# A decoding pass that writes back in place, and a planner that counts a locked pass in full

## The chip, the cores and the metric

The kernel runs on one core of one Trainium2 chip. The metric is the device time of one execution in microseconds (us). Three executions of the kernel before took 615.13, 615.44 and 616.31 us; the median is 615.44.

## What is computed

The reference chains a chunked linear recurrence with decay (a state-space layer) and two dense feed-forward layers:

```python
for c in range(nc):                       # attention part, per batch and head
    cum = np.cumsum(la, axis=-1)
    M = np.einsum('bhin,bhjn->bhij', Cc, Bc) * np.exp(cum_i - cum_j) * causal
    y = np.einsum('bhij,bhjd->bhid', M, xc) + (Cc @ state) * np.exp(cum)
    state = decay_full * state + sum_j(Bc_j xc_j decay_from_j)
x = y as 3072 tokens x 256
h = x @ w_in;  x = (h * sigmoid(1.702 * h)) @ w_out       # first layer, 256 -> 2048 -> 256
h = x @ w_in2; x = (h * clip(h + 3, 0, 6) / 6) @ w_out2   # second layer
```

Everything is in float32.

## The kernel before

**Tiling.** The sequence is cut into 8 chunks of 96 steps. A chunk c has 4 pieces, one per batch, so there are 32 pieces q = 4c + b. A piece needs two decay scans on VectorE (`decay`, L387), eight small matmuls for the scores (`s_mm`, L458, named S below), two products scores times decay (`g_mul` on VectorE, L461, or `g_copy` on ScalarE and `g_pool` on GpSimd, L464 and L468), sixteen small matmuls (`y_mm`, L479, named Y), and then `y_out` on ScalarE (L487) and `y_lo` on VectorE (L492), which write the piece into a token block `xt`.

The two feed-forward layers go over seven token blocks of 384 or 480 columns (A is the first layer, B the second). The inner loop has 16 units m per block and layer; a unit is four plus two matmuls `l1` (L615) and six `l2` (L654). Every float32 operand is split into a rounded high part and the rest, so that three products are summed: `wh` and `wl` for a weight, `gh` and `gl` for an activation. The first twelve units are all of block 0; after them block 0 and block 1 alternate, so block 1 (pieces q4 to q7) must be there when unit 12 is under way.

**Weights.** There are 32 weight tiles p, one per unit and layer. They arrive as 64-bit words and are decoded on the chip in five steps:

- `w_load` (L295): a DMA of 512 KB into one of three buffers `raw`, as pairs of a low and a high 32-bit word.
- `w_scale` (L300, ScalarE): the high words, scaled, are written to one of two buffers `dec`.
- `w_low` (L305, VectorE): the low words are shifted, in place in `raw`.
- `w_join` (L309, VectorE): `dec` shifted and joined with the low words, in place in `dec`. It is the last reader of `raw`.
- `w_top` (L312, ScalarE) writes `wh` from `dec`; `w_bottom` (L318, GpSimd) writes `wl` from `dec` and `wh`. It is the last reader of `dec`.

**What sets the order.** The order of all instructions on the five engines comes out of the planner `Schedule`. Each operation is added with an engine, a planned duration, a due time (`key`), what it reads and writes (`r`, `w`) and which pool buffer it takes (`new`). `run` goes through planned time and takes on each engine the ready operation with the earliest due time. An operation that takes a buffer can't be planned before that buffer is free. An operation with `port=True` on VectorE, and each one on GpSimd, is lengthened in the plan if the other engine is in such an operation at that time. On the chip every engine and SyncE, which issues nearly all DMAs, go through their lists strictly in order, each instruction waiting for semaphores.

Of the kernel before, what the change touches and what calls it, by code (L numbers as in the profile page):

```python
# [8 lines left out]
F32 = mybir.dt.float32  # L9
# [5 lines left out]
AF = mybir.ActivationFunctionType  # L15
ALU = mybir.AluOpType
# [60 lines left out]
class Schedule:  # L77
# [12 lines left out]
    def add(self, eng, dur, key, fn, *args, r=(), w=(), new=(), kb=0, after=0.0, port=False):  # L90
        self.ops.append(dict(eng=eng, dur=dur, key=key, fn=fn, args=args, r=list(r), w=list(w) + list(new),
                             new=list(new), kb=kb, port=port or eng == "POOL", n=len(self.ops), ready=max(after, key - 8) if kb else after))
# [5 lines left out]
    def run(self):  # L98
# [39 lines left out]
        port = {"DVE": 0.0, "POOL": 0.0}  # L138
        pipe = 0.0
        order = []  # L140
        while any(cand.values()):
            best = None
            for e, cs in cand.items():
                run = []
                for o in cs:
                    t, need = max(at[e], o["ready"]), {}
                    for x in o["new"]:
                        p = x.split(":")[0]
                        need[p] = need.get(p, 0) + 1
                    for p, k in need.items():  # L150
                        f = sorted(free[p])
                        mine = set(turn[p][:k]) <= set(o["new"])
                        t = max(t, f[k - 1][0]) if mine and len(f) >= k else None
# [7 lines left out]
                t, k, n, o = min((x for x in run if x[0] <= t0 + 0.02), key=lambda x: x[1:3])  # L161
                for x in sorted(run, key=lambda x: x[1:3]):

                    if x[1] + 3 < k and x[0] <= t + min(0.4 * o["dur"], 0.5):
                        t, k, n, o = x
# [5 lines left out]
            t, n, o = best  # L171
            e = o["eng"]
            cand[e].remove(o)
            for x in o["new"]:
                f = free[x.split(":")[0]]
# [4 lines left out]
            if o["port"]:  # L180

                other = "DVE" if e == "POOL" else "POOL"
                o["dur"] += (0.45 if e == "POOL" else 0.6) * max(0.0, min(port[other] - t, o["dur"]))
                port[e] = t + o["dur"]
            at[e] = t + o["dur"]
            if o["kb"]:
# [25 lines left out]
def ssd_moe_kernel(ctx: ExitStack, tc: tile.TileContext, xs, aa, bc, bcz_d, bc0, wu, pat, idn, out):  # L212
    nc = tc.nc
# [3 lines left out]
    add = sch.add  # L217
# [39 lines left out]
    def B_(x):  # L257
        p = x.split(":")[0]
        return {"raw": raw_b, "dec": dec_b, "l": l_b, "gm": gm_b, "xs": xs_b, "st": st_b, "xt": xt_b, "gg": gg_b,
                "gh": gh_b, "gl": gl_b, "r16": r16_b, "lx": lx_b, "scr": scr_b, **banks}[p][sch.slot[x]]  # L260
# [19 lines left out]
    tu, t = [], START  # L280
# [8 lines left out]
    for q in range(NC * NB):  # L289
        k = max(i for i in range(NK) if LO[i] <= CH * q)  # L290
# [6 lines left out]
    def w_scale(p):  # L297


        nc.scalar.activation(B_(f"dec:{p}").bitcast(F32), B_(f"raw:{p}")[:, :, 1].bitcast(F32), AF.Prelu,  # L300
                             scale=2.0 ** 16, alpha=2.0 ** 32)

    def w_low(p):
        low = B_(f"raw:{p}")[:, :, 0]
        nc.vector.tensor_scalar(low, low, 29, None, ALU.logical_shift_right)  # L305

    def w_join(p):
        t = B_(f"dec:{p}")
        nc.vector.scalar_tensor_tensor(t, t, 3, B_(f"raw:{p}")[:, :, 0], ALU.logical_shift_left, ALU.bitwise_or)  # L309

    def w_top(p, e):
        (e.copy if e is nc.scalar else e.tensor_copy)(w_hi[p], B_(f"dec:{p}").bitcast(F32))  # L312
# [203 lines left out]
    for q in range(NC * NB):  # L516
        c, b = divmod(q, NB)
        t = kp[q]
        blk, f = block[q]
        if c in ROWS and b == 0:  # L520
            sch.take(rname(c), t - 5 if c else -75)
            rows[c] = []
            for i in range(4):
                for s in range(2) if c != 1 else (None,):
                    e = "SP" if c or s else "ACT"
                    n = f"r16.{c}.{i}.{s}"
                    add(e, 0.84 if c > 1 else 0.42, t - 4 if c else -70 + i, r16_load, {"SP": nc.sync, "ACT": nc.scalar}[e], c, i, s,
                        r=[rname(c)], w=[n], kb=115 if c == 1 else 57)
# [61 lines left out]
    for p in range(2 * NM):  # L590
        k = tu[first[p]] - 1.5
        R, Dn = f"raw:{p}", f"dec:{p}"
        n0 = 2 * NM - LATE
        add("SP", 0.4, k - 9, w_load, p, new=[R], kb=512, after=(2.9, 4.9, 6.9)[p] if p < 3 else 0.0)
        add("ACT", 0.72, k - 1.6, w_scale, p, r=[R], new=[Dn])
        add("DVE", 0.45, k - 1.9, w_low, p, w=[R], port=True)
        add("DVE", 0.70, k - 1.0, w_join, p, r=[R], w=[Dn], port=True)
        e = TOP(p)
        add(e, {"ACT": 0.64, "DVE": 0.43, "POOL": 1.0}[e], k - 0.5, w_top, p, ENG[e], r=[Dn], w=[f"wh{p}"])
        late_r, late_w = ["late"] * (p > n0), ["late"] * (p == n0)  # L600
        e = BOT(p)
        add(e, {"DVE": 0.78, "POOL": 1.3}[e], k, w_bottom, p, ENG[e], r=[Dn, f"wh{p}"] + late_r, w=[f"wl{p}"] + late_w, port=True)
# [174 lines left out]
```

## Time and profile before

| | |
|---|---|
| median of three executions | 615.44 us (615.13 to 616.31) |
| the profiled execution | 615.93 us, of which the span of the profile is 614.1 us |
| PE (TensorE matmul) busy | 601.0 us, 98% |
| VectorE (DVE) busy | 310.4 us, 51% |
| ScalarE (ACT) busy | 310.3 us, 51% |
| GpSimd (POOL) busy | 207.1 us, 34% |
| DMA | 53.69 MB, mean 87 GB/s |

TensorE is busy nearly all of the span, so time can be won or lost only where it stands still or runs at a lower granted clock. A stretch of the timeline shows for each instruction its start, its length and, in square brackets, how long its engine stood idle before it and what ended that wait. The lengths of VectorE and GpSimd include time in which the instruction was issued and not yet let through.

### The profile page before, as it was taken

To read this page: it belongs to the slowest core of one execution; us is meant where nothing else is said; L and a number is where in the kernel's file an instruction comes from. 1 tells how busy PE (TensorE), PEld (TensorE's weight loads), DVE (VectorE), ACT (ScalarE), POOL (GpSimd) and SP (SyncE) were. 2 spreads that over 40 slices of the span, in tenths; PEclk is the share of its full clock that TensorE was granted. 3 is DMA by queue.
4 is the path that set the end of the run, shared out by engine and by line. 5 is a ranking of instruction groups with operands and counts; after the bars stand their busy time and mean duration, and the time that the engine had idled before them with its cause. 6 is when DMAs were issued, how large, how long until landed. Compare 5 with 4: busy or idle time off the path is not lost.

```text
span 614.1 us, 9456 instructions
## 1 busy us (share of the span) xinstructions
PE 601.0 (98%) x3628; PEld 530.6 (86%) x3628; DVE 310.4 (51%) x466; ACT 310.3 (51%) x624; POOL 207.1 (34%) x176
## 2 busy tenths in 40 slices
PE   9787999999999999999999999999999999999997
PEld 7676998999998898788888888888888899988997
DVE  5979988654564777533545533644423222232222
ACT  3556666666555444444544446344445444444443
POOL 3646413264352551002750005550004430044453
PEclk9889899999999999999999999999999999999999
DMA  8676644434114492340425301903000010000000
GB/s 227 139 221 220 184 152 130 143 103 143 57 42 130 152 245 61 104 122 1 122 52 149 112 2 29 234 1 119 1 0 1 0 34 2 0 1 1 32 2 26
DMA packets 46781, 53.69 MB, mean 87 GB/s; under 512 B 27296, under 2 KB 38160, under 8 KB 46736
## 3 DMA queue, kind: packets, MB, share of 16 engines
q1 hardware_dynamic: 45888, 52.74, 30.0%
q10 hardware_dynamic: 848, 0.35, 0.3%
q8 instruction: 28, 0.46, 0.3%
q14 instruction: 17, 0.14, 0.1%
HBM read 42.01 MB, written 10.60 MB: 86 GB/s over the span
## 4 chain that ended last, share of the span: by engine, by line
PE 93%; DMA 2%; DVE 2%; ACT 1%; issue 1%; POOL 0%; SPq 0%; ACTq 0%; DVEq 0%; POOLq 0%
PE h L615 43%; PE acc L654 43%; PE s L458 2%; PE y L479 2%; PE acc L375 1%; DMA late<-in_bc 1%; PE s L479 1%; DMA raw<-in_wu 1%; DVE dec L309 1%; DVE l L387 1%; PE h L458 1%; PE acc L458 0%; PE y L335 0%; DVE gl L640 0%; DVE raw L305 0%
## 5 line engine op out<-in xcount | busy, mean ns | idle before, releaser
L640 POOL TENSOR_TENSOR gl<-gg,gh 128x480 fp32r<-128x480 f32 (+1 forms) x111 | 133.2, 1202 | 315.8 <-ACT gh L630 285.8
L615 PE MATMUL h<-xt,wh 128*128 128x480 f32 (+1 forms) x896 | 220.2, 368 | 2.5 <-DVE xt L492 1.5
L615 PEld LDWEIGHTS h<-xt,wh 128*128 128x128 f32 x896 | 162.9, 190 | 21.1 <-issue 3.5
L654 PE MATMUL acc<-gh,wh 128*128 128x384 f32 (+1 forms) x448 | 162.7, 363 | 0.0
L635 DVE SCALAR_TENSOR_TENSOR gg<-gg,h 128x480 f32<-128x480 f32 (+1 forms) x112 | 68.2, 609 | 142.3 <-ACT gg L628 142.0
L654 PE MATMUL acc<-gl,wh 128*128 128x384 f32 (+1 forms) x448 | 128.5, 363 | 2.0 <-DVE gl L640 2.0
L640 DVE TENSOR_TENSOR gl<-h,gh 128x480 fp32r<-128x480 f32 (+1 forms) x112 | 68.5, 611 | 121.5 <-ACT gh L630 99.6
L654 PE MATMUL acc<-gh,wl 128*128 128x480 f32 (+1 forms) x322 | 118.1, 367 | 0.0
L626 ACT ACTIVATE h<-h 128x480 f32<-128x480 f32 (+1 forms) x112 | 58.4, 521 | 111.2 <-PE h L615 111.0
L628 ACT ACTIVATE gg<-h 128x480 f32<-128x480 f32 (+1 forms) x112 | 60.3, 538 | 78.3 <-PE h L615 75.9
L630 ACT CAST gh<-gg 128x480 fp32r<-128x480 f32 (+1 forms) x112 | 62.6, 559 | 60.8 <-DVE gg L635 60.4
L615 PE MATMUL h<-xt,wl 128*128 128x480 f32 (+1 forms) x322 | 91.5, 365 | 1.8 <-POOL wl L318 1.8
L654 PEld LDWEIGHTS acc<-gl,wh 128*128 128x128 f32 x448 | 83.3, 189 | 10.2 <-DVE gl L640 2.6
L654 PEld LDWEIGHTS acc<-gh,wh 128*128 128x128 f32 x448 | 84.7, 189 | 7.5
L387 DVE TENSOR_TENSOR_SCAN l<-l,pat_sb 112x448 f32<-112x448 f32 x56 | 78.8, 1421 | 3.2 <-DMA l<-acl_d 3.1
L615 PEld LDWEIGHTS h<-xt,wl 128*128 128x128 f32 x322 | 59.5, 189 | 9.2 <-POOL wl L318 3.4
L654 PEld LDWEIGHTS acc<-gh,wl 128*128 128x128 f32 x322 | 61.0, 189 | 6.2 <-issue 0.8
L630 ACT CAST gh<-h 128x480 fp32r<-128x480 f32 (+1 forms) x112 | 58.9, 526 | 4.4
L318 POOL TENSOR_TENSOR wl<-dec,wh 128x512 fp32r<-128x512 f32 x23 | 36.1, 1582 | 58.2 <-ACT wh L312 58.2
L654 PE MATMUL acc<-gh,w_late 128*128 128x480 f32 (+1 forms) x126 | 45.8, 363 | 0.0
L615 PE MATMUL h<-xt,w_late 128*128 128x480 f32 (+1 forms) x126 | 35.2, 360 | 0.0
L309 DVE SCALAR_TENSOR_TENSOR dec<-dec,raw 128x512 uint32<-128x512 uint32 x32 | 28.9, 903 | 2.9 <-ACT dec L300 1.2
(67 smaller groups left out, 376.1 us busy)
## 6 DMA issues: line engine op xcount, KB each, us to landing
raw<-in_wu SPq DMA_DIRECT2D x32, 512.0 KB, 4.2
l<-acl_d SPq DMA_DIRECT2D x28, 392.0 KB, 4.3
st<-scr SPq DMA_DIRECT2D x8, 896.0 KB, 5.4
scr<-tsplit SPq DMA_DIRECT2D x32, 168.0 KB, 2.9
xs<-in_xs SPq DMA_DIRECT2D x8, 384.0 KB, 4.9
out<-gg SPq DMA_DIRECT2D x10, 192.0 KB, 2.7
scr<-tsplit SPq DMA_DIRECT2D x16, 112.0 KB, 3.3
raw<-in_bc SPq DMA_DIRECT2D x4, 384.0 KB, 5.1
```

What stands on the lines that cost most here:

```text
L309: nc.vector.scalar_tensor_tensor(t, t, 3, B_(f"raw:{p}")[:, :, 0], ALU.logical_shift_left, ALU.bitwise_or)
L318: e.tensor_tensor(out=w_lo[p], in0=B_(f"dec:{p}").bitcast(F32), in1=w_hi[p].bitcast(F32), op=ALU.subtract)
L387: nc.vector.tensor_tensor_scan(t, a, pat_sb, 0.0, ALU.mult, ALU.add)
L458: nc.tensor.matmul(out=ps[:, k, :], lhsT=l, rhs=r, start=True, stop=True)
L479: nc.tensor.matmul(out=yv[32 * k:32 * k + 32, g, :], lhsT=x[:, b, h * D:(h + 1) * D], rhs=B_(f"gm:{q}.{g}")[:, k, :], start=True, stop=True)
L615: nc.tensor.matmul(out=ps, lhsT=w[p][:, 128 * j:128 * j + 128], rhs=x[:, xp, j, 0:n], start=not lo and (xp, j) == (1, 0), stop=lo and j == 1)
L626: nc.scalar.activation(ps, ps, AF.Gelu_apprx_sigmoid)
L628: nc.scalar.activation(B_(f"gg:{u}")[:, 0:n], ps, AF.Relu, bias=3.0)
L630: nc.scalar.copy(B_(f"gh:{u}")[:, 0:n], ps if kind == "A" else B_(f"gg:{u}")[:, 0:n])
L635: nc.vector.scalar_tensor_tensor(out=g, in0=g, scalar=6.0, in1=B_(f"h:{u}")[:, 0:n], op0=ALU.min, op1=ALU.mult)
L640: e.tensor_tensor(out=B_(f"gl:{u}")[:, 0:n], in0=g, in1=B_(f"gh:{u}")[:, 0:n].bitcast(F32), op=ALU.subtract)
L654: nc.tensor.matmul(out=acc[d], lhsT=w[p][:, 256 + 128 * d:384 + 128 * d], rhs=g, start=(m == 0 and d not in seen), stop=(m == NM - 1 and d ...
```

## The change

`w_scale` writes its result over the high words of `raw` rather than to `dec`. `w_join` reads both words from `raw` and writes `dec`, so that it is now `w_join` that takes the `dec` buffer. In the planner the dependences follow: `w_scale` and `w_low` each only read `raw` as a whole and have names of their own (`hi`, `low`), `w_join` waits for both. Apart from that, the planner's rule for operations on the shared port adds the whole rest of the other engine's operation; it was 0.45 or 0.6 of it, and at most that share of the operation's own length.

```diff
@@ Schedule.run
             if o["port"]:
                 other = "DVE" if e == "POOL" else "POOL"
-                o["dur"] += (0.45 if e == "POOL" else 0.6) * max(0.0, min(port[other] - t, o["dur"]))
+                o["dur"] += max(0.0, port[other] - t)
                 port[e] = t + o["dur"]
@@ decoding
     def w_scale(p):
-        nc.scalar.activation(B_(f"dec:{p}").bitcast(F32), B_(f"raw:{p}")[:, :, 1].bitcast(F32), AF.Prelu,
-                             scale=2.0 ** 16, alpha=2.0 ** 32)
+        top = B_(f"raw:{p}")[:, :, 1].bitcast(F32)
+        nc.scalar.activation(top, top, AF.Prelu, scale=2.0 ** 16, alpha=2.0 ** 32)
...
     def w_join(p):
-        t = B_(f"dec:{p}")
-        nc.vector.scalar_tensor_tensor(t, t, 3, B_(f"raw:{p}")[:, :, 0], ALU.logical_shift_left, ALU.bitwise_or)
+        t = B_(f"raw:{p}")
+        nc.vector.scalar_tensor_tensor(B_(f"dec:{p}"), t[:, :, 1], 3, t[:, :, 0], ALU.logical_shift_left, ALU.bitwise_or)
@@ planner entries
-        add("ACT", 0.72, k - 1.6, w_scale, p, r=[R], new=[Dn])
-        add("DVE", 0.45, k - 1.9, w_low, p, w=[R], port=True)
-        add("DVE", 0.70, k - 1.0, w_join, p, r=[R], w=[Dn], port=True)
+        add("ACT", 0.72, k - 1.6, w_scale, p, r=[R], w=[f"hi{p}"])
+        add("DVE", 0.45, k - 1.9, w_low, p, r=[R], w=[f"low{p}"], port=True)
+        add("DVE", 0.70, k - 1.0, w_join, p, r=[R, f"hi{p}", f"low{p}"], new=[Dn], port=True)
```

No instruction is added or taken away; VectorE has 460 rows of program before and after. What changes is the order on all engines, at three places as follows.

VectorE, from the low activation part `gl` of unit 3 of block 0 on, before. L305 and L309 are `w_low` and `w_join`; the first pair here is weight 5, the second weight 6. The buffer `l1` holds the decay of piece q5, `l2` that of q6, and `gm2`, `gm3` take the products of q5.

```order
L640 TENSOR_TENSOR gl0_152<-h0_158,gh0_149 128x384
L461 TENSOR_TENSOR gm0_137<-s0_164,l0_134 112x448
L387 SCALAR_TENSOR_TENSOR l1_135<-l1_135,pat_sb_68 112x448
L305 TENSOR_SCALAR raw2_131<-raw2_131 128x512
L309 SCALAR_TENSOR_TENSOR dec1_133<-dec1_133,raw2_131 128x512
L640 TENSOR_TENSOR gl1_153<-h1_159,gh1_150 128x384
L461 TENSOR_TENSOR gm2_139<-s0_164,l1_135 112x448
L305 TENSOR_SCALAR raw0_129<-raw0_129 128x512
L309 SCALAR_TENSOR_TENSOR dec0_132<-dec0_132,raw0_129 128x512
L492 TENSOR_TENSOR xt1_145<-y0_165,xt1_145 128x2x96
L461 TENSOR_TENSOR gm3_140<-acc3_163,l1_135 112x448
L387 SCALAR_TENSOR_TENSOR l2_136<-l2_136,pat_sb_68 112x448
```

The first scan of q5 stands a few rows further up, so both scans of q5 and one of its products come before the join of weight 6. The same place after the change, from the row behind the same `gl0`:

```order
L305 TENSOR_SCALAR raw2_131<-raw2_131 128x512
L309 SCALAR_TENSOR_TENSOR dec1_133<-raw2_131 128x512
L305 TENSOR_SCALAR raw0_129<-raw0_129 128x512
L640 TENSOR_TENSOR gl1_153<-h1_159,gh1_150 128x384
L309 SCALAR_TENSOR_TENSOR dec0_132<-raw0_129 128x512
L305 TENSOR_SCALAR raw1_130<-raw1_130 128x512
L492 TENSOR_TENSOR xt1_145<-y0_165,xt1_145 128x2x96
L309 SCALAR_TENSOR_TENSOR dec1_133<-raw1_130 128x512
L640 TENSOR_TENSOR gl2_154<-h0_158,gh2_151 128x384
L305 TENSOR_SCALAR raw2_131<-raw2_131 128x512
L387 SCALAR_TENSOR_TENSOR l1_135<-l1_135,pat_sb_68 112x448 x2
L309 SCALAR_TENSOR_TENSOR dec0_132<-raw2_131 128x512
```

Both scans of q5 now stand behind the join of weight 7, and its two products come later still.

SyncE, the DMA queue around the load of weight 5, before (`l` are the decay rows of a piece, `late` the rows of the second chunk, `xs1<-st_tr` moves the state on):

```order
L381 DMA l1_135<-acl_d_155 112x896
L295 DMA raw1_130<-in_wu 128x1024
L430 DMA late_128<-in_bc0 16x1792 x4
L500 DMA xs1_142<-st_tr_71 16x8x32 x4
L295 DMA raw2_131<-in_wu 128x1024
L381 DMA l2_136<-acl_d_155 112x896
L295 DMA raw0_129<-in_wu 128x1024
L295 DMA raw1_130<-in_wu 128x1024
```

After:

```order
L381 DMA l1_135<-acl_d_155 112x896
L430 DMA late_128<-in_bc0 16x1792
L295 DMA raw1_130<-in_wu 128x1024
L430 DMA late_128<-in_bc0 16x1792 x3
L500 DMA xs1_142<-st_tr_71 16x8x32 x4
L381 DMA l2_136<-acl_d_155 112x896
L295 DMA raw2_131<-in_wu 128x1024
L295 DMA raw0_129<-in_wu 128x1024
L295 DMA raw1_130<-in_wu 128x1024
```

One of the four `late` loads goes ahead of weight 4 (the first `raw1`), and the decay rows of q6 go ahead of weight 5 (`raw2`). The loads of weights 6 and 7 have the same transfers ahead of them as before.

ScalarE, around `wh5`, before:

```order
L626 ACTIVATE h1_159<-h1_159 128x384
L630 CAST gh1_150<-h1_159 128x384
L300 ACTIVATE dec0_132<-raw0_129 128x512
L312 CAST wh5_78<-dec1_133 128x512
L483 COPY st_sb_70<-y0_165 128x2x16
L487 CAST xt1_145<-y0_165 128x2x96
L312 CAST wh6_79<-dec0_132 128x512
```

After:

```order
L626 ACTIVATE h1_159<-h1_159 128x384
L630 CAST gh1_150<-h1_159 128x384
L301 ACTIVATE raw0_129<-raw0_129 128x512
L312 CAST wh5_78<-dec1_133 128x512
L483 COPY st_sb_70<-y0_165 128x2x16
L487 CAST xt1_145<-y0_165 128x2x96
L312 CAST wh6_79<-dec0_132 128x512
```

Here only the operand of the scaling pass changes: that of weight 6 stands ahead of `wh5` in both.

## Rows read from the trace of the kernel before

**Rows 1.** Windows of 20 us: time, busy of PE, PEld, DVE, ACT, POOL, granted clock, DMA.

```profile
40.00:60.00 20.00, 16.35 (x129) 13.81 (x130) 18.16 (x27) 13.84 (x30) 11.81 (x8) 0.98 0.62 207
60.00:80.00 20.00, 19.77 (x125) 18.44 (x125) 18.61 (x27) 12.24 (x26) 8.11 (x5) 0.91 0.62 179
80.00:100.00 20.00, 20.00 (x158) 18.43 (x157) 16.06 (x29) 12.56 (x29) 4.94 (x4) 1.00 0.54 174
...
580.00:600.00 20.00, 20.00 (x116) 20.00 (x115) 5.55 (x10) 9.98 (x21) 9.30 (x10) 1.00 0.07 23
```

**Rows 2.** Timeline of PE: start, length, instruction, idle time ahead of it and its releaser.

```profile
37.30 0.48 PE L479 MATMUL y<-gm,xs 112*32 112x112 f32 x8 [1.14 <-POOL gm L468]
...
39.87 1.43 PE L615 MATMUL h<-xt,wh 128*128 128x384 f32 x4
...
46.62 0.97 PE L615 MATMUL h<-xt,wh 128*128 128x384 f32 x4 [0.98 <-ACT wh L312]
...
59.79 0.62 PE L654 MATMUL acc<-gl,wh 128*128 128x384 f32 x2 [1.98 <-DVE gl L640]
...
67.20 0.86 PE L615 MATMUL h<-xt,wh 128*128 128x384 f32 x4
```

**Rows 3.** Timeline of ScalarE.

```profile
17.26 0.53 ACT L464 COPY gm<-h 112x448 f32<-112x448 f32 x1 [1.55 <-PE h L458]
...
34.77 0.69 ACT L300 ACTIVATE dec<-raw 128x512 f32<-128x512 f32 x1 [1.96 <-DMA raw<-in_wu]
...
38.61 0.71 ACT L300 ACTIVATE dec<-raw 128x512 f32<-128x512 f32 x1 [1.84 <-DMA raw<-in_wu]
39.21 0.61 ACT L312 CAST wh<-dec 128x512 fp32r<-128x512 f32 x1
```

**Rows 4.** Timeline of VectorE.

```profile
33.08 2.05 DVE L387 TENSOR_TENSOR_SCAN l<-l,pat_sb 112x448 f32<-112x448 f32 x1
...
35.57 0.69 DVE L309 SCALAR_TENSOR_TENSOR dec<-dec,raw 128x512 uint32<-128x512 uint32 x1
...
37.27 0.61 DVE L461 TENSOR_TENSOR gm<-s,l 112x448 f32<-112x448 f32 x1
...
39.34 0.69 DVE L309 SCALAR_TENSOR_TENSOR dec<-dec,raw 128x512 uint32<-128x512 uint32 x1 [0.37 <-ACT dec L300]
...
49.31 1.57 DVE L309 SCALAR_TENSOR_TENSOR dec<-dec,raw 128x512 uint32<-128x512 uint32 x1
...
57.34 1.08 DVE L387 TENSOR_TENSOR_SCAN l<-l,pat_sb 112x448 f32<-112x448 f32 x1
...
65.57 0.36 DVE L492 TENSOR_TENSOR xt<-y,xt 128x192 fp32r<-128x192 f32 x1 [0.24 <-ACT st_sb L483]
```

**Rows 5.** Groups of VectorE from 39 to 66 us: busy, mean ns, idle before.

```profile
L309 DVE SCALAR_TENSOR_TENSOR dec<-dec,raw 128x512 uint32<-128x512 uint32 x8 | 8.8, 1100 | 0.8 <-ACT dec L300 0.4
L387 DVE TENSOR_TENSOR_SCAN l<-l,pat_sb 112x448 f32<-112x448 f32 x4 | 7.1, 1786 | 0.0
L640 DVE TENSOR_TENSOR gl<-h,gh 128x384 fp32r<-128x384 f32 x7 | 3.8, 548 | 1.4 <-ACT gh L630 1.4
L305 DVE TENSOR_SCALAR raw<-raw 128x512 uint32<-128x512 uint32 x7 | 2.9, 408 | 0.0
```

**Rows 6.** Timeline of GpSimd: a pass that meets no VectorE pass.

```profile
60.00 1.30 POOL L318 TENSOR_TENSOR wl<-dec,wh 128x512 fp32r<-128x512 f32 x1 [3.84 <-ACT wh L312]
```

**Rows 7.** Groups of GpSimd from 39 to 66 us.

```profile
L318 POOL TENSOR_TENSOR wl<-dec,wh 128x512 fp32r<-128x512 f32 x8 | 13.4, 1685 | 12.1 <-ACT wh L312 12.1
```

**Rows 8.** Groups by shape over the whole span.

```profile
L300 ACT ACTIVATE dec<-raw 128x512 f32<-128x512 f32 x32 | 21.7, 678 | 10.8 <-DMA raw<-in_wu 6.2 <-POOL wl L318 4.6
...
L312 ACT CAST wh<-dec 128x512 fp32r<-128x512 f32 x32 | 19.7, 622 | 5.0 <-DVE dec L309 4.6
```

**Rows 9.** Timeline of SyncE's DMA issues: start, time until the last issue of the row.

```profile
29.42 0.35 SPq L295 DMA_DIRECT2D raw<-in_wu  x1
30.41 0.32 SPq L381 DMA_DIRECT2D l<-acl_d  x1
31.22 1.71 SPq L295 DMA_DIRECT2D raw<-in_wu  x2
```

## The prediction

> **What bounds the kernel now.** I read the windows first, then PE's timeline, then the engines that PE waits for. The windows [rows 1] show where there is anything to win: from 80 us on PE is busy in all of every window at full clock, and it stays so up to 600 us. Between 40 and 60 us it is busy 16.35 of 20 us, and between 60 and 80 us 19.77 at a granted clock of 0.91, which lacks 20 x 0.09 = 1.8 us of full speed. So the time is decided before about 67 us, and what is won or lost there goes to the end one for one.
>
> PE's timeline [rows 2] gives the points by which I measure. Unit 5 of block 0 starts at 39.87. The second block (layer A, block 1, unit 0) starts at 67.20; after that nothing waits. Between them PE stands still for 0.98 us (for `wh7` of ScalarE) and 1.98 us (for a low part `gl` of VectorE), and there are shorter stops for `wl` of GpSimd.
>
> Who sets 39.87? ScalarE's timeline [rows 3]: the cast to `wh5` begins at 39.21 and takes 0.61, so it ends at 39.82, and 0.05 later unit 5 starts. Ahead of it in ScalarE's list stands the scaling pass of weight 6, which waited 1.84 us for its DMA until 38.61. Weight 5 itself had landed before 34.77 [rows 3] and was joined from 35.57 on [rows 4], some 3 us earlier. So the landing of weight 6 sets 39.87, and PE's own stop of 1.14 us at 37.30 [rows 2] lies in its shadow.
>
> From 40 us on VectorE decides. Its join of weight 6 ends at 40.03; the low part of piece q7, the last of the second block's tokens, starts at 65.57 [rows 4]. That is 25.5 us, and the groups of that stretch [rows 5] show it full: joins, scans, low parts and shifts, with idle time of 0.8 + 1.4 us in the first three groups, of which 0.4 precedes the join of weight 6. Some of that busy time is waiting. A join takes 0.69 us alone and 1.57 us when a GpSimd pass is running, a scan takes 1.08 alone and up to 2.05 [rows 4]. Over the stretch the mean join is 1.100 and the mean scan 1.786 us [rows 5], so the waiting is 8 x (1.10 - 0.69) + 4 x (1.79 - 1.08) = 3.3 + 2.8 = 6.1 us. The other side pays too: a `wl` pass takes 1.30 us alone [rows 6] and 1.685 in the mean [rows 7].
>
> **The change, part by part.**
>
> *ScalarE's scaling pass, 32 times.* Same instruction, another target: strided words in place of a contiguous tile. No row shows ScalarE writing with this stride. As bounds I take the contiguous cast of the same size, 0.622 us, and as much above today's 0.678 as that lies below, 0.73 [rows 8]: 32 x 0.056 = 1.8 us either way on an engine that is busy for half the span and waits for others in this stretch. I take nothing.
>
> *It no longer waits for a `dec` buffer.* That wait is 4.6 us of ScalarE's idle time in all [rows 8]. It moves to the join on VectorE, whose list is then blocked in its place, with the low parts, products and scans behind it. Where a GpSimd pass holds the buffer it would mostly have held up the join anyway. I take nothing for it by itself; if all of it were on PE's path it would give back up to 4.6 us.
>
> *The join reads two strided words.* It already reads one with that stride, at 0.69 us [rows 4], and shift passes with a strided source and target take 0.41 [rows 5]. Between nothing and, if a second strided source cost as much as the first pass over it, 0.41 x 7 = 2.9 us up to the second block, I take nothing, since the join row is the nearest.
>
> *Before 40 us.* The scaling of weight 2 now runs ahead of a ScalarE copy for which ScalarE had been idle for 1.55 us [rows 3]: free. The shift pass of weight 2 runs ahead of the join of weight 1, which puts the first unit back by at most 0.41 us [rows 5]. On SyncE the decay rows of q6 go ahead of weight 5: they were issued at 30.41, weight 5 at 29.42 [rows 9], so weight 5 comes about 1 us later. All this ends in the shadow of weight 6. Its load was issued at 31.22, first of two [rows 9], behind the same bytes as after the change, and its scaling still stands ahead of `wh5`. So unit 5 starts at about 39.9 again: nothing, with 1 us either way if the landing shifts.
>
> *Between 40 us and the second block.* Here is the cost. Before, VectorE did both scans and one product of q5 before 40 us, while it waited for weights: the second scan at 33.08, the product at 37.27 [rows 4]. In the new list the shift passes of weights 5 and 6 stand ahead of them, and these wait for DMAs that landed just before 34.77 and 38.61 us [rows 3]. VectorE waits with them, and the scans and the product come after the join of weight 7. So the stretch from the join of weight 6 to the low part of q7 holds the same joins, shifts, low parts and pieces as before, and in addition two scans and one product: 2 x 1.08 + 0.53 = 2.7 us (0.53 because the next instruction starts 0.08 before the 0.61 of a product are over).
>
> The waiting need not stay at 6.1 us. Its lower bound is nothing; the upper one is that each of the eight `wl` passes holds up a VectorE pass in full, 8 x 1.30 = 10.4. To choose I walked the new list by hand with the durations above. The join of weight 7 meets the `wl` pass of weight 6, the second scan of q5 that of weight 7, the second scan of q6 that of weight 9, a join that of weight 10, and the two scans of q7 the GpSimd product and the `wl` of weight 11: six meetings of about 1 us. So I keep 6.1, and the idle time as well. What is late next is weight 8, whose join comes some 2 us later than before in that walk, and with it unit 8; weight 7 is earlier.
>
> **The sum.** 0 + 0 + 0 + 2.7 = 2.7 us: the second block starts at about 69.9 and all later ones follow. Against the profiled execution, 615.93 us (span 614.1 and 1.83 around it), that is 618.6; the median of the runs is 0.49 lower, so I predict 618.1. Bounds of that term: waiting at nothing gives 2.7 - 6.1 = -3.4, waiting in full 2.7 + 4.3 = +7.0.
>
> **A rule against this reading.** A VectorE join beside a GpSimd pass takes 1.57 us, its own 0.69 and the rest of the other's 1.30 [rows 4, 6]; nothing looks like sharing. The Trainium skill says so too (SBUF — State Buffer, "Who interferes with whom"): two-source VectorE instructions and GpSimd reads take turns under an exclusive lock, and whoever comes second blocks fully. By that rule the planner's old share of 0.6 was wrong and the new one is right, so its order should avoid meetings and the sum would be that of the faster rival below. That the old order's waiting is 6.1 us of 25.5 is in favour of it.
>
> **The rivals.** A measurement of this kernel can tell about 0.2% from no change, 1.2 us.
>
> *Faster: the fuller account avoids the meetings.* The planner now sees that a join behind a GpSimd pass costs the whole rest, and puts shifts and low parts there. Were waiting to fall to about 1 us, the result is 2.7 - 5.1 = -2.4, 613.0 us. It decides from a waiting of 6.1 - 2.7 - 1.2 = 2.2 us downwards. For it: the old account was clearly too small. Against it: the plan does not know that weights 4 to 7 land late, so its passes don't stand side by side as planned. Chance 0.25.
>
> *No change.* Waiting between 2.2 and 4.6 us, or the shifted scans fall into gaps like the 1.4 us before a low part [rows 5]: 614.2 to 616.6, around 615.4. Chance 0.18.
>
> *Clearly slower: stops of PE lower the clock again.* After the stop of 1.98 us the granted clock of 60 to 80 us is 0.91 [rows 1, 2]. In my walk there is a stop of similar length for weight 12. If it comes in addition to one like the old, another 1.8 us are lost: 618.1 + 1.8 = 619.9; with two more meetings 622. Chance 0.15.
>
> That the scaling gains nothing because it shares its tile with the shift pass, and the two take turns, I exclude: in the new program the shift still waits for nothing but its load.
>
> **How the numbers follow.** The forecast, +2.7 at waiting between 4.9 and 7.5 us, 616.9 to 619.5, has a chance of 0.42. With the clearly slower case that makes 0.57 for slower, 0.18 for no change and 0.25 for faster. The range leaves out the far part of the faster case, and of the clearly slower one: 612.8 to 621.0.
>
> **What would show it.** Right: unit 5 again at 39.9 us; VectorE idle for several us between 33 and 39, waiting for `raw`; both scans of q5 after 43 us; six scans rather than four in the groups between the join of weight 6 and q7, with a mean near 1.6 to 1.8 us; the second block at about 69.9; PE full from there. Wrong: unit 5 well before 39 us, which would mean that the landing of weight 6 is not what holds it; means of joins and scans close to 0.7 and 1.1 us, which is the faster rival; a second block on time with PE idle later, which would put the loss into pieces of later chunks.

## The result and the profile after

The changed kernel takes 621.36 us in the median of four executions (621.15 to 623.7), beside 615.46 for the kernel before (615.13 to 616.31): a ratio of 1.0102, with a 95% interval of 1.0076 to 1.0129. It is 5.9 us slower; the forecast was 2.7 us slower, with a range that ended at 621.0. The execution in the profile took 621.22 us, 619.4 of it span, so the span grew by 5.3.

The windows of 20 us, against [rows 1] (same columns):

```profile
40.00:60.00 20.00, 15.38 (x106) 11.90 (x106) 17.20 (x24) 11.11 (x24) 8.80 (x5) 0.91 0.65 181
60.00:80.00 20.00, 17.80 (x111) 16.19 (x112) 13.94 (x20) 10.45 (x23) 7.46 (x6) 0.83 0.53 157
80.00:100.00 20.00, 19.84 (x147) 18.42 (x146) 17.48 (x29) 12.01 (x26) 2.79 (x2) 1.00 0.41 133
```

PE is less busy in both stretches, its granted clock is lower in both, and VectorE, which I had expected to fill up, is idler: 31.1 us of 40 rather than 36.8. PE's timeline, against [rows 2]:

```profile
37.12 1.85 PE L615 MATMUL h<-xt,wh 128*128 128x384 f32 x8
...
46.62 0.97 PE L615 MATMUL h<-xt,wh 128*128 128x384 f32 x4 [0.60 <-ACT wh L312]
48.52 0.62 PE L615 MATMUL h<-xt,wl 128*128 128x384 f32 x2 [0.93 <-POOL wl L318]
...
57.80 0.62 PE L615 MATMUL h<-xt,wl 128*128 128x384 f32 x2 [0.83 <-POOL wl L318]
...
64.90 1.65 PE L615 MATMUL h<-xt,wh 128*128 128x384 f32 x4 [2.14 <-DVE gl L640]
...
71.81 0.86 PE L615 MATMUL h<-xt,wh 128*128 128x384 f32 x4
```

Unit 5 starts at 37.12, 2.75 us earlier than before. The second block starts at 71.81, 4.6 later. Four matmuls that take 0.97 us at 46.62 take 1.65 at 64.90: the second set runs at half clock. The granted clock is 0.50 from 65 to 71 us, and it is 0.50 from 52 to 54 us too.

For each kernel of this study I added up two things from its profile: the idle times in brackets on PE's timeline from 33 to 80 us ("stops"), and 10 x (1 - granted clock) over the five windows of 10 us from 30 to 80 ("clock"), which is the full-speed time lost there. "Block 2" is the start of the second block; "rest" is the span less that, and hardly varies. Each line is one execution. Before 30 us the executions differ too: from 20 to 30 us the granted clock is 0.83 in the kernel before and in the change and 0.66 to 0.71 in the other six, so differences of a microsecond between these lines carry no reading.

| kernel | unit 5 | unit 12 | block 2 | stops | clock | span | rest |
|---|---|---|---|---|---|---|---|
| before | 39.87 | 64.98 | 67.20 | 5.0 | 3.5 | 614.1 | 546.9 |
| the change | 37.12 | 64.90 | 71.81 | 7.8 | 5.2 | 619.4 | 547.6 |
| e2, old port rule | 37.09 | 60.86 | 63.76 | 4.9 | 0.0 | 611.5 | 547.7 |
| e9, copies first | 38.11 | 64.20 | 68.19 | 6.8 | 1.7 | 615.8 | 547.6 |
| e10, and scans early | 37.91 | 61.68 | 67.17 | 6.2 | 1.7 | 614.9 | 547.7 |
| e12, e2 with scaling ahead | 37.06 | 62.44 | 66.51 | 6.5 | 1.7 | 614.7 | 548.2 |
| e14, e2 with bank first | 36.15 | 58.23 | 61.48 | 2.8 | 0.0 | 609.4 | 547.9 |
| e15, change with bank first | 39.19 | 61.62 | 66.17 | 6.5 | 0.0 | 615.0 | 548.8 |

The change adds 2.8 us of stops and 1.7 of clock, together 4.5: the 4.6 by which the second block is late. The 2.75 us won at unit 5 are gone by unit 12, which starts at the same time as before. Of the change's 5.2 us of clock, 1.7 are lost at 51 to 54 us and 3.5 behind the stop at unit 12. PE's list differs there too: the sixteen Y of a piece and one more set of six `l2`, about 1.6 us of work at full clock, stand behind the first matmuls of unit 12 after the change and ahead of them before.

VectorE's groups from 39 to 72.5 us, against [rows 5]:

```profile
L387 DVE TENSOR_TENSOR_SCAN l<-l,pat_sb 112x448 f32<-112x448 f32 x6 | 9.1, 1535 | 0.0
L309 DVE SCALAR_TENSOR_TENSOR dec<-raw 128x512 uint32<-128x512 uint32 x8 | 7.1, 889 | 0.2
...
L305 DVE TENSOR_SCALAR raw<-raw 128x512 uint32<-128x512 uint32 x7 | 3.5, 496 | 0.0
...
L492 DVE TENSOR_TENSOR xt<-y,xt 128x192 fp32r<-128x192 f32 x3 | 1.1, 357 | 3.8 <-ACT xt L487 2.7 <-ACT st_sb L483 1.0
```

Six scans rather than four, as foreseen. The waiting for GpSimd fell: 8 x (0.889 - 0.69) + 6 x (1.535 - 1.08) = 4.3 us where I kept 6.1. The seven shift passes, which hardly waited before, add 0.6 (0.496 in the mean rather than 0.408). VectorE stood idle instead, for 3.8 us ahead of low parts of pieces (`y_lo`).

### The profile page after: what moved, and what is told of

The parts are those of the page before. It is cut to its first block, busy times and chain, and to the rows that moved or that the text cites. A ratio compares the mean times of both kernels' runs of the same rounds, so it can differ in the third digit from the quotient of the medians.

```text
span 619.4 us, 9446 instructions
## 1 busy us (share of the span) xinstructions
PE 603.8 (97%) x3628; PEld 531.6 (86%) x3628; DVE 306.1 (49%) x466; ACT 308.4 (50%) x624; POOL 207.6 (34%) x176
## 4 chain that ended last, share of the span: by engine, by line
PE 88%; DMA 4%; DVE 3%; issue 2%; POOL 1%; ACT 1%; SPq 0%; POOLq 0%; DVEq 0%
PE h L615 41%; PE acc L654 41%; DMA raw<-in_wu 2%; PE s L458 2%; PE y L479 1%; DMA late<-in_bc 1%; DVE l L387 1%; PE s L479 1%; POOL wl L318 1%; PE acc L375 1%; POOL gm L468 1%; DVE dec L309 1%; PE acc L458 0%; PE y L335 0%; DMA scr<-tsplit 0%
## 5 line engine op out<-in xcount | busy, mean ns | idle before, releaser
L387 DVE TENSOR_TENSOR_SCAN l<-l,pat_sb 112x448 f32<-112x448 f32 x56 | 71.7, 1293 | 0.4 <-DMA l<-acl_d 0.4
L402 POOL TENSOR_TENSOR raw<-raw,tsplit 128x384 f32<-128x384 f32 x8 | 7.4, 922 | 96.2 <-ACT tsplit L397 93.5
```

The source lines that it names most:

```text
L387: nc.vector.tensor_tensor_scan(t, a, pat_sb, 0.0, ALU.mult, ALU.add)
L402: nc.gpsimd.tensor_tensor(out=t[:, s] if i == 0 else tsplit[:, 2, s, :, 0:CH], in0=t[:, s], in1=d, op=ALU.subtract)
```

## The experiments

A ratio is to executions of the kernel before that were taken beside the run; their medians are 614.28 to 614.76 us, so runs are compared by their ratios. Each ratio has its 95% interval behind it.

### Which half of the change: planner, instructions, or both (e1, e2, e3)

**e1** takes only the planner's rule into the kernel before:

```diff
-                o["dur"] += (0.45 if e == "POOL" else 0.6) * max(0.0, min(port[other] - t, o["dur"]))
+                o["dur"] += max(0.0, port[other] - t)
```

> Only the planner's port rule is changed, the decoding is that of before. Theory A (the loss comes from VectorE's list: scans of q5 put behind the joins of weights that land late, so that two scans and a product fall into the stretch after 37 us): here one scan of q5 stands ahead of the join of weight 5 and one behind that of weight 6, so about half of the loss, 617 to 619 us. Theory B (the loss comes from the join being the one that waits for a dec buffer): nothing of it here, 612.5 to 615.5, with unit 5 at about 37 us by the earlier DMAs.

619.35 us, ratio 1.006 (1.0037 to 1.0083): just above the range of theory A, and far from B. The fuller account did cut the waiting. VectorE's groups in e1 from 39 to 70 us:

```profile
L309 DVE SCALAR_TENSOR_TENSOR dec<-dec,raw 128x512 uint32<-128x512 uint32 x8 | 7.0, 875 | 0.1
L387 DVE TENSOR_TENSOR_SCAN l<-l,pat_sb 112x448 f32<-112x448 f32 x5 | 6.9, 1379 | 0.0
```

That is 8 x (0.875 - 0.69) + 5 x (1.379 - 1.08) = 3.0 us rather than 6.1, and the kernel is slower all the same.

**e2** is the changed kernel with that line as it was.

> Only the decoding is changed (in place, the join takes the buffer), with the planner's old port rule. Here both scans of q5 stand ahead of the join of weight 5. Theory A: no loss, and if the earlier DMAs bring unit 5 to about 37 us some of that gain is kept, 612.5 to 615.5. Theory B: the loss is here, 618 to 622.

612.91 us, ratio 0.9969 (0.995 to 0.9988): faster than the kernel before. Its trace shows full clock in every window from 30 us on.

**e3** has the new `w_scale` and `w_join` in the kernel before, with every planner line, and so the order, left as it was.

> The new instructions in the old order (planner as before, only the bodies of the scaling and joining passes are new). If the instructions themselves cost nothing, as predicted: within 0.7 us of before, joins of 0.69 us alone, scaling passes of 0.68 us. If the strided target or the join's wait for the buffer costs: 616.5 or more.

614.96 us, ratio 1.0004 (0.9984 to 1.0024). The groups by shape, whole span, of e3 (the scaling pass, then the join):

```profile
L301 ACT ACTIVATE raw<-raw 128x512 f32<-128x512 f32 x32 | 21.7, 678 | 5.2 <-DMA raw<-in_wu 5.2
L309 DVE SCALAR_TENSOR_TENSOR dec<-raw 128x512 uint32<-128x512 uint32 x32 | 29.3, 917 | 3.7 <-ACT raw L301 1.5
```

The scaling pass takes 678 ns, the very figure of [rows 8], so the strided target costs nothing that can be measured here. The join takes 917 ns where it took 903 over the whole span. All of the change's time that can be measured is order. The two halves of it do not add up: -0.31% for the new dependences and +0.60% for the port rule make +0.29%, and together they cost 1.02%. Something in the combination is worth about 0.7%, or 4.5 us.

### The early start (e4)

The kernel before, with the two DMAs moved as the change moves them (`r16_load` is the load of the `late` rows, `a_load` that of the decay rows):

```diff
+    ahead(at(r16_load, nc.sync, 1, 0), at(w_load, 4))
+    ahead(at(a_load, 6), at(w_load, 5))
```

> The kernel before with two DMAs moved as the change moves them: one of the four loads of the second chunk's rows ahead of weight 4, the decay rows of q6 ahead of weight 5. If these two moves are why unit 5 started 2.75 us earlier in the changed kernel: unit 5 at about 37.1 us here too, and the end at 612.7 to 614.5. If the earlier start there came from the order of the other engines: unit 5 at 39.9 and 615.4.

617.24 us, ratio 1.003 (1.0001 to 1.0058), ten executions from 613.92 to 619.78: outside both ranges. Unit 5 starts earlier than in the kernel before. But it does so in e3 as well, whose order is that of the kernel before. First e4, then e3:

```profile
37.92 0.87 PE L615 MATMUL h<-xt,wh 128*128 128x384 f32 x4
```

```profile
38.36 0.96 PE L615 MATMUL h<-xt,wh 128*128 128x384 f32 x4 [0.66 <-ACT wh L312]
```

So unit 5 starts at 39.87 and 38.36 in two executions of the old order, at 37.92 with the two DMAs moved, and between 37.12 and 39.32 (e5) in the changed kernel and the kernels made from it with its order of DMAs. That the DMA order makes the early start, and how much of the 2.75 us, is not shown. In the changed kernel SyncE issues the loads of weights 5 to 7 so (against [rows 9], where weight 7 left at 32.93):

```profile
25.90 0.59 SPq L500 DMA_DIRECT2D xs<-st_tr  x1
27.74 0.32 SPq L381 DMA_DIRECT2D l<-acl_d  x1
28.67 2.38 SPq L295 DMA_DIRECT2D raw<-in_wu  x3
```

The three loads are issued one after another from 28.67 to 31.05; weight 6 leaves at 29.67 rather than 31.22, and ScalarE's pass for it no longer waits for its load:

```profile
34.33 0.70 ACT L301 ACTIVATE raw<-raw 128x512 f32<-128x512 f32 x1 [2.17 <-DMA raw<-in_wu]
...
35.81 0.71 ACT L301 ACTIVATE raw<-raw 128x512 f32<-128x512 f32 x1
36.40 0.61 ACT L312 CAST wh<-dec 128x512 fp32r<-128x512 f32 x1
```

In the kernel before and in e3 a state transfer in SyncE's queue waits 2.2 and 2.0 us for a weight's load ahead of these issues; with the DMAs moved no such wait is seen. Between 28 and 32 us the DMA engines moved 78 and 125 GB/s in windows of 2 us before, and 105 and 262 after, but their busy share was 0.75 and 1.10 before and 0.98 and 1.00 after. So whether the queue of issues or the transfers under way held weight 6 back stays open. An early start alone wins nothing here: e4 is no faster than the kernel before.

### VectorE's list (e5, e6, e7)

These start from the changed kernel and move operations on VectorE's list. A line below names what is moved, and the operation ahead of which it is put.

```diff
+  decay(5, both halves)  ->  ahead of w_low(5)       # e5
+  y_lo(5)                ->  ahead of w_join(10)     # e6
+  y_lo(6)                ->  ahead of w_join(12)     # e6
```

**e5** puts both scans of q5 back ahead of the first shift pass that waits for its load, the step from which the prediction took its 2.7 us.

> The changed kernel with one move: both scans of q5 go back ahead of the shift pass of weight 5 on VectorE. Theory A (their place behind the joins of weights 5 to 7 is what costs): VectorE has 2.2 us less to do after unit 5, so the second block starts some 2 to 3 us earlier than 71.8 and the end is at 617.5 to 619.5. Theory C (what costs is that VectorE's list is blocked by the low parts of q5 and q6, which wait for TensorE and ScalarE): no change, 620.5 to 622.

619.95 us, ratio 1.0098 (1.0082 to 1.0115), between the two ranges: no gain that can be told from the change's 1.0102.

**e6** lets two low parts of pieces, ahead of which VectorE stood idle, follow one operation later.

> The changed kernel with two moves on VectorE: the low parts of q5 and q6, before which it stood idle for 0.76 and 1.95 us, go behind the scan that follows them. Theory A: VectorE waits elsewhere, within 1 us of the changed kernel. Theory C: the joins of weights 10 and 12 come up to 2.7 us earlier, unit 12 starts near 63 us rather than 64.9, and the end is at 617 to 619.5.

621.65 us, ratio 1.0127 (1.011 to 1.0144). **e7** does both.

> Both moves together. If A and C are two parts of the loss they add up: 614 to 617. If they are one and the same (VectorE's list as a whole is late), it is no better than the better of the two, 617 to 619.5.

620.95 us, ratio 1.0107 (1.0088 to 1.0126), slower than either theory had it. So my term for the scans, put right, gains nothing by itself. Why it doesn't is in the traces. ScalarE's timeline and then PE's in e5 (here L682 is the activation, L686 `gh`, L357 `w_scale`, L368 `w_top`, L671 `l1`):

```profile
61.23 0.47 ACT L682 ACTIVATE h<-h 128x384 f32<-128x384 f32 x1 [1.46 <-PE h L671]
61.73 0.48 ACT L686 CAST gh<-h 128x384 fp32r<-128x384 f32 x1
63.51 0.67 ACT L357 ACTIVATE raw<-raw 128x512 f32<-128x512 f32 x1 [1.30 <-DMA raw<-in_wu]
64.08 0.61 ACT L368 CAST wh<-dec 128x512 fp32r<-128x512 f32 x1
```

```profile
64.74 0.97 PE L671 MATMUL h<-xt,wh 128*128 128x384 f32 x4 [3.55 <-ACT wh L368]
```

The scans came earlier, weight 12 was joined by 62.05, and PE stood still for 3.55 us all the same, because the copy to `wh12` stands behind the scaling pass of weight 14, and that waits for its load. In e6 the same pass waits 2.55 us and the stop is 4.82. The changed kernel shows it too, at weight 10 and at weight 14:

```profile
45.39 0.68 ACT L301 ACTIVATE raw<-raw 128x512 f32<-128x512 f32 x1 [0.86 <-DMA raw<-in_wu]
45.97 0.60 ACT L312 CAST wh<-dec 128x512 fp32r<-128x512 f32 x1
...
62.80 0.47 ACT L626 ACTIVATE h<-h 128x384 f32<-128x384 f32 x1 [1.28 <-PE h L615]
63.30 0.48 ACT L630 CAST gh<-h 128x384 fp32r<-128x384 f32 x1
63.68 0.67 ACT L301 ACTIVATE raw<-raw 128x512 f32<-128x512 f32 x1
64.24 0.61 ACT L312 CAST wh<-dec 128x512 fp32r<-128x512 f32 x1
```

The copy at 45.97 is `wh8`, whose join ended at 44.88; 1.1 us late, and the stops of 0.60 and 0.93 us at unit 8 come from it.

### Matmuls that only keep PE busy (e8)

The changed kernel, with twenty matmuls of no use ahead of unit 12; they add work, and their result is not read.

> The changed kernel with 20 matmuls of no use put ahead of unit 12 of the first block, where TensorE stood still for 2.14 us before its clock went to half for 7 us (65 to 71 us). Their result is written to a free bank and read by nothing. Theory D (the stop brings the half clock, and the half clock is worth about 3 us): granted clock 1.00 from 64 to 72 us, second block at about 69, end at 618 to 619.5. If the clock falls anyway, or falls for another reason: 621 to 623.

620.14 us, ratio 1.0096 (1.0077 to 1.0116), between the two ranges. PE did them before the copy was there, and then waited:

```profile
60.47 2.36 PE L666 MATMUL y<-pat_sb 112*128 112x256 bf16 x20
65.10 0.97 PE L678 MATMUL h<-xt,wh 128*128 128x384 f32 x4 [2.27 <-ACT wh L368]
```

The clock from 60 to 70 us is 0.83 in this trace (0.73 in the changed kernel's): this settles nothing about the clock, since a stop of the same length was still there.

### Scaling passes ahead of copies (e9 to e12)

In the order before, the scaling pass of weight p took the `dec` buffer that the passes of weight p - 2 release, so it could not stand ahead of the copy of weight p - 2. Now it waits only for its load. On ScalarE's list of the changed kernel the scaling passes of weights 6, 10 and 14 stand ahead of the copies of weights 5, 8 and 12; in the kernel before only that of weight 6 does, and in e2 none of the three. So it takes both halves of the change to put those of 10 and 14 there. **e9** is the changed kernel with this:

```diff
+  w_top(5)   ->  ahead of w_scale(6)
+  w_top(8)   ->  ahead of w_scale(10)
+  w_top(12)  ->  ahead of w_scale(14)
```

> The change, with three copies of ScalarE (high halves of weights 5, 8 and 12) put ahead of the scaling pass that the change's order puts in front of each (weights 6, 10 and 14); nothing else moves. Theory A (those passes wait for a weight's load, 0.86 us at 45.39 in the changed kernel and 1.3 to 2.6 us in the kernels with scans or low-half subtractions moved, and hold up a copy that is ready): ScalarE shows no wait for a load ahead of these copies, unit 8's stop of 0.60 and the low-half stop of 0.93 behind it shrink by about 1 us together, unit 12's stop of 2.14 by 0.5, so 1 to 2 us less alone, 3 to 4 if the half clock of 64 to 72 us goes too: 617.5 to 620.5. Theory B (VectorE's list alone sets it): 620.5 to 622.5, unit 12 at 64.9 as before.

618.42 us, ratio 1.0069 (1.0044 to 1.0094): 0.33%, 2.0 us, off the change, with intervals that overlap. None of the three copies waits behind a load any more. **e10** has the scans of q5 early in addition,

> The same three copies first, and both scans of the sixth piece ahead of the shift pass of weight 5 (as in the earlier kernel with the scans alone, 619.95). Theory A: the stop before unit 12 was 3.55 us there, behind a copy that waited for the scaling pass of weight 14 and its load; the copy can now go at about 62.1, the product that frees the bank at 63.05, so unit 12 starts near 63.1, its stop is 1.5 to 2.2 and the second block starts at 65.5 to 67.5: 614 to 617.5. Theory B (the order of ScalarE does not matter): 619 to 621.

and takes 616.75 us, ratio 1.0045 (1.0026 to 1.0064). The scans alone were worth nothing (e5, 1.0098); behind the moved copies they may count, 0.24% from e9 to e10, with intervals that overlap. The three copies take 0.53% off e5, 3.3 us, with intervals far apart. **e11** has the low parts later as well.

> The same, and the two low-half subtractions of the sixth and seventh pieces one scan later. Theory A: unit 12 at 62 to 63.5, no wait of ScalarE for a load ahead of a copy: 613.5 to 617.5, at most what the kernel with copies and scans alone takes, plus or minus 1. Theory B: 619 to 622, as the kernel with both VectorE moves (620.95).

617.96 us, ratio 1.0046 (1.0028 to 1.0063), half a microsecond above what I had allowed; the low parts do not matter.

**e12** is the converse: e2, the fast kernel, with `w_scale(10)` ahead of `w_top(8)` and `w_scale(14)` ahead of `w_top(12)`.

> The converse: the fast kernel (the change without the planner's new port rule, 612.91), with the scaling passes of weights 10 and 14 put ahead of the copies of weights 8 and 12, as in the changed kernel. Theory A: the passes wait for their loads or at least take 0.6 us ahead of each copy; unit 12 starts 0.6 to 2.5 us later than 60.9; 613.5 to 617.5. Theory B: the same time as the fast kernel within 0.8 us, 612 to 613.6.

616.43 us, ratio 1.0021 (1.0001 to 1.0042), 0.52% or 3.2 us above e2. ScalarE and PE in e12, at weight 10 and unit 8:

```profile
46.60 0.67 ACT L356 ACTIVATE raw<-raw 128x512 f32<-128x512 f32 x1 [1.68 <-DMA raw<-in_wu]
47.17 0.60 ACT L367 CAST wh<-dec 128x512 fp32r<-128x512 f32 x1
```

```profile
47.83 0.44 PE L670 MATMUL h<-xt,wh 128*128 128x384 f32 x1 [2.19 <-ACT wh L367]
```

And in e2, where the copy goes first:

```profile
45.57 0.62 ACT L312 CAST wh<-dec 128x512 fp32r<-128x512 f32 x1 [0.63 <-DVE dec L309]
...
47.03 0.68 ACT L301 ACTIVATE raw<-raw 128x512 f32<-128x512 f32 x1
```

Nothing else was moved. Two such passes put into the order of e2 cost 3.2 us; three taken out of the changed kernel's are worth 3.3 us with the scans early, and 2.0 us, not clear of noise, without.

### The stop before unit 12 (e13 to e16)

Unit 12 writes the bank of unit 10, so it also waits for VectorE's low part `gl` of unit 10. The profile puts the stop of 2.14 us down to it, but it ended at 63.90; the copy to `wh12` ended at 64.85, 0.05 before unit 12 starts, so the copy came last. It stood behind unit 11's activation and `gh` and the scaling pass of weight 14; it could not go before the join at 62.24 was done, and in the changed kernel that join stands behind a low part of a piece and a scan, and `gl` behind the join:

```profile
60.96 0.36 DVE L492 TENSOR_TENSOR xt<-y,xt 128x192 fp32r<-128x192 f32 x1 [1.95 <-ACT xt L487]
61.24 1.08 DVE L387 TENSOR_TENSOR_SCAN l<-l,pat_sb 112x448 f32<-112x448 f32 x1
62.24 0.67 DVE L309 SCALAR_TENSOR_TENSOR dec<-raw 128x512 uint32<-128x512 uint32 x1
62.82 0.61 DVE L461 TENSOR_TENSOR gm<-s,l 112x448 f32<-112x448 f32 x1
63.35 0.55 DVE L640 TENSOR_TENSOR gl<-h,gh 128x384 fp32r<-128x384 f32 x1
```

Three moves take it out. In e13 they are added to e10, in **e15** they are made alone in the changed kernel, and in e14 they are made in e2 (with the scan of q7 in place of `y_lo(6)`):

```diff
+  g_lo(unit 10)  ->  ahead of y_lo(6)
+  w_join(12)     ->  ahead of y_lo(6)
+  w_top(12)      ->  ahead of act(unit 11)
```

> The same three moves alone in the changed kernel (621.36), whose stop before unit 12 is 2.14 us at 64.90 with the half clock behind it to 72 us. Theory A: unit 12 starts at 62.7 to 63.6, 1.3 to 2.1 earlier; the half clock after it costs up to 4 us more, which goes if the stop set it off and stays if the earlier stops (0.46, 0.83) did: 615.5 to 620. Theory B (the stop is not set by these three places): 620.5 to 622.5.

616.62 us, ratio 1.0035 (1.0012 to 1.0058): 0.67%, or 4.1 us, of the change's 1.02% are gone. The three moves were not made one by one, so what each is worth is not shown; the third also takes `wh12` out from behind the scaling pass of weight 14. PE in e15, and the window behind it:

```profile
61.62 0.96 PE L671 MATMUL h<-xt,wh 128*128 128x384 f32 x4 [0.58 <-ACT wh L368]
```

```profile
60.00:70.00 10.00, 9.10 (x71) 7.40 (x70) 8.36 (x15) 5.78 (x14) 3.28 (x3) 1.00 0.87 241
```

The stop shrank from 2.14 to 0.58 and the clock of 60 to 70 us rose from 0.73 to 1.00. The second block starts at 66.17, a microsecond earlier than in that trace of the kernel before (65.53 in e3, which has its order). The 1.7 us of clock at 51 to 54 us are not there in this trace either, and they lie ahead of anything that was moved.

> The change with the three copies first and both scans of the sixth piece early (616.75), and in addition, ahead of the eighth piece's second scan on VectorE, the subtraction that frees unit 10's bank and the join of weight 12, and the copy of weight 12 ahead of unit 11's activation on ScalarE. Theory A (the stop before unit 12 is made of list order alone, and the half clock of 63 to 67 us comes with it): the bank is free at about 58.5 and the copy ends at 59.8 to 60.2, so the stop of 2.00 shrinks to 0 to 0.5, the second block starts 2 to 4 us earlier than 67.2, 612.5 to 615. Theory B (something else, a load or GpSimd, is next in line): the stop stays above 1.3 and the time at 616 or more.

616.47 us, ratio 1.0023 (1.001 to 1.0036), more than theory A allowed. The stop shrank to 0.58 and the second block starts at 65.64, but the rest is 550.2 us rather than 547.7: two new stops, 0.61 at 68.53 and 1.12 at 76.94, come behind it.

> The same three moves in the fast kernel (the change without the port rule, 612.91), whose stop before unit 12 is 1.68 us at 60.86. Theory A: the stop shrinks to 0 to 0.5 and the time by 0.8 to 1.7: 611 to 612.3. Theory B: 612.5 to 614.

611.5 us, ratio 0.9945 (0.9929 to 0.9962). This is the fastest kernel of the study, and beats the kernel before and the changed one. Its stop before unit 12 went from 1.68 to 0.38.

What is left of the change in e15 lies behind the second block in this trace. ScalarE's timeline of e15 there:

```profile
64.05 0.69 ACT L357 ACTIVATE raw<-raw 128x512 f32<-128x512 f32 x1 [1.59 <-DMA raw<-in_wu]
...
67.92 0.68 ACT L357 ACTIVATE raw<-raw 128x512 f32<-128x512 f32 x1 [1.61 <-DMA raw<-in_wu]
```

The first is weight 14, issued at 60.73 behind ten small loads. **e16** puts it ahead of them.

```diff
+  w_load(14)  ->  ahead of the ten r16_load that stand in front of it
```

> The changed kernel with the three moves before unit 12 (616.62), and SyncE's load of weight 14 ahead of the ten small loads that stood in front of it (issued at 56.1 to 60.6, weight 14 at 60.73). What is left over the kernel before (about 2 us) comes behind the second block's start, where ScalarE waits 1.59 us for weight 14 at 64.05 and PE stops 1.12 us at 76.13. Theory A (these late loads are the rest): weight 14 is issued at 57 or earlier, the wait at 64.05 goes, the stop at 76.13 shrinks, 614 to 616. Theory B (the rest is elsewhere, or the small loads, now later, take its place): 616.2 to 618.

619.45 us, ratio 1.0088 (1.0072 to 1.0105): slower, and outside both ranges. The wait for weight 14 went, the one for weight 15 behind it grew to 3.25 us (at 67.56), and the stop of 1.12 us stayed, at 75.76. The profiled execution is the shortest of the five, 616.4, so its trace does not show where the other 3 us of the median lie. Where the last third of a per cent of e15 comes from stays open.

## Why the prediction was right or wrong

*The bound.* Right. Whatever was done, the rest from the second block on took 546.9 to 550.2 us, and the time was decided before. In e13, e15 and e16 (548.8 to 550.2) new stops lie behind that point.

*"So unit 5 starts at about 39.9 again: nothing."* Wrong for the profiled execution, by 2.75 us in favour of the change. I took the load of weight 6 to leave as before, "behind the same bytes"; it left 1.55 us earlier, and the pass for it no longer waited. But I had one trace of the old order, and e3, with the same order, starts unit 5 at 38.36. How much of the 2.75 us is the change's stays open.

*The instructions at nothing.* Right: e3 measures 1.0004, and the scaling pass takes what it took.

*"It no longer waits for a `dec` buffer ... I take nothing for it by itself."* This is the step that failed. I asked where the wait goes, and found it on VectorE's join. I did not ask where the instruction goes: without that wait the planner may put it ahead of work that is ready, and what stands ahead of work on a list in strict order passes its own wait on. I looked at the one place where the order was the same (weight 6 ahead of `wh5`), and not at weights 10 and 14. The term that I put at nothing measured 3.2 us for those two passes (e12 against e2), and 3.3 us for the three (e10 against e5); taken out of the changed kernel alone, the three gave 2.0 us, not clear of noise (e9).

*"2 x 1.08 + 0.53 = 2.7 us".* The two scans did come late, VectorE did wait for `raw` before them (2.02 us ahead of the shift at 34.33), and the count of six was right. But the term is not the loss: taking it away alone gains nothing (e5). Behind the moved copies the scans are worth 0.24% between e9 and e10, 1.5 us, with intervals that overlap.

*"So I keep 6.1, and the idle time as well."* Wrong in both. The waiting fell to 4.3 us, into the span of the rival without a change. A join beside a GpSimd pass still takes 1.50 us (at 38.91). The exclusive lock that I weighed there from the Trainium skill (SBUF — State Buffer, "Who interferes with whom") agrees with that row. But the idle time rose by more: VectorE was idle for 8.9 of the 40 us rather than 3.2. In e1, with the planner's rule alone, the waiting fell to 3.0 us and the time rose by 0.6%. A better account of one cost did not make a better order; which places of e1's order cost the time was not followed up.

*The rival "stops of PE lower the clock again".* Its term came out, and I gave it 0.15: I had 1.8 us of clock for one more stop, and the traces show 1.7 more than before. That its whole, 2.7 + 1.8 = 4.5 us, is also the 4.5 that I added up in the traces is luck in the other part: its 2.7 were two scans and a product, and what was there were 2.8 us of stops that have other causes. Most of the half clock followed the stop of 2.14 us, and with the stop at 0.58 it did not come: the mean granted clock of the change's four executions is 0.984 to 0.989, that of e15's eight 0.993 or 0.994 but for one at 0.989.

The direction came out right, by another road than the one I gave, and the size was half of what it is: of the change's 1.02%, 0.67% hang on the three places before unit 12, and the remainder is not located.

## What to carry to other kernels

When a change takes a wait away from an instruction, look where the order will now put that instruction, on every list and at every repetition, and what stands ready behind it: a pass that waits for a DMA held up a ready copy behind it, by 1.1 us at weight 8 in the changed kernel. If the order comes from a planner, measure the two parts of a change (the dependences and the cost rule) apart and together; here the one gained 0.3%, the other lost 0.6%, and both lost 1.0%. And a stop of PE of 2 us can cost as much again in the clock behind it (3.5 us behind the one of 2.14 here, nothing in the traced execution of e4), so the work that frees the next unit's bank and weight goes first.

## What was not expected of the hardware

How much the granted clock decides between executions of one program: those three of e4 at a mean clock of 0.996 take 613.92 to 614.04 us, the five at 0.985 or 0.986 take 617.86 to 619.78. I had taken the clock for a small correction. It does not order the times of every program: e2 took 613.13 us at 0.997 and 613.08 at 0.988. Between the traces of e2 and of the kernel before it is the larger term: e2's second block starts 3.4 us earlier, with stops of the same sum (4.9 and 5.0 us), and full clock was granted from 30 us on. Half of that can be the execution: e3, with the order of the kernel before, lost 1.7 us of clock rather than 3.5 and starts its second block at 65.53. In the window of 60 to 70 us the granted clock is 0.83 in the kernel before, 0.70 in e7, 0.83 in e12 and 0.66 in e11, where PE stood still for 1.98, 2.14, 1.93 and 2.26 us in or shortly before it; it is 1.00 in e2, e9 and e15, where that stop was 1.68, 1.59 and 0.58 us. But it is 1.00 also in the profiled execution of e4, with a stop of 1.98 us at 59.03, so the same stop brings the half clock in some executions and not in others. And in the changed kernel the half clock at 51 to 54 us came behind stops of 0.69, 0.60 and 0.93 us, so the length of one stop does not decide it. Useless matmuls ahead of a stop did not prevent it (e8).
